# Softmax division moved from GpSimd to ScalarE, and a plan with other transfer rules and weights

## The chip, the cores and the metric

The kernel runs on one core of a Trainium2 chip. Its engines have queues of their own and run them in order: TensorE (PE), VectorE (DVE), ScalarE (ACT), GpSimd (POOL) and SyncE (SP), which issues most transfers (DMA). The metric is the device time of one execution in microseconds (us), less is better.

## The reference

Three parts in a row, all in float32. First attention with 2 batches x 8 heads, 576 rows and a head width of 64, in which each row keeps its 32 largest scores:

```python
scores = scale * np.matmul(q, k.transpose(0, 1, 3, 2))
kth = np.partition(scores, -top_k, axis=-1)[..., -top_k:-top_k + 1]   # top_k = 32
scores = np.where(scores >= kth, scores, -1e9)
attn = np.exp(scores - scores.max(-1, keepdims=True))
attn = attn / (attn.sum(-1, keepdims=True) + 1e-9)
out = np.matmul(attn, v)
```

Then an MLP on the 1152 x 512 result, `h = x @ w_in; (h * cos(h)) @ w_out`, with 2048 hidden columns and weights that come as 64-bit floats. Last a layer of 8 experts: each row goes to the expert with the largest gate logit (a capacity of 288 rows each), `relu(x @ w1) @ w2` with 1024 hidden columns, times the gate's probability.

## The kernel before, in words

The program writes down operations with engine, cost, inputs and outputs (`P.op`, `P.dma`), and a planner (`Plan.emit`) then plays a schedule through with these costs: at each turn it takes, over all engines, the operation that can start first, with ties broken by a rank, and issues it there and then. The order in which it picks is the order in each engine's queue. The ranks come from a table of numbers, `PRM` (the main path) or `FULL` (a fallback that this input does not need). The planner holds VectorE and GpSimd apart for operations marked `port=True`.

Attention is 36 steps (`steps`), each one tile of 128 rows for two heads. A step is:

- `scores` (L477, L483): two halves of matmuls into the one PSUM tile `S`, each copied to `Sp` by ScalarE (L489). There are four `Sp` buffers, so copies run up to three steps ahead.
- `pair_chain`, the search: VectorE takes the larger and the smaller of column pairs (L504, both inputs in SBUF), and alternates "largest 8" (L508, L517, L519) with "replace those 8" (L512).
- `softmax`: the threshold `tb` (GpSimd, L544, L547), a penalty `pen` (ScalarE, L551), its subtraction (GpSimd, L554), the exponential with row sums (ScalarE, L556), a small addition (GpSimd, L559), the reciprocal (VectorE, L561), and the division by the sums, one instruction for each of the two halves (L566): on GpSimd for the first 25 steps and on VectorE for the other 11.
- `products`: nine transposes on TensorE (L581), copies by ScalarE (L583), matmuls with `v`, a copy of the result `xh` on ScalarE (L633) and its rounding rest `xl` on VectorE (L626).

Between these stand the first MLP's parts. `convert` turns 32 tiles of 64-bit weights into float32: a transfer into `wraw` (three buffers), a pass on ScalarE (L384), and then one of two forms. For tiles n < `mul` VectorE does all the rest (L388, L390, L393); for the others ScalarE makes signs (L397), VectorE assembles the bits (L398, L400) and GpSimd multiplies (L403). `split_w` splits 16 of the tiles in a rounded part (L360 on ScalarE, or L358 on GpSimd) and a rest (L354, on VectorE for n < `lod`, else on GpSimd). `layer_in` (L676 to L678, clamp on VectorE, L687), `cosine` (ScalarE, L704), `product` (GpSimd, L712) and `layer_out` (L721) are the MLP; `route` and `place` choose experts. After the last search step TensorE finishes the MLP, rows are gathered by expert, and the experts follow (from L938 on).

```python
eng = DVE if on_dve else POOL
P.op("dve" if on_dve else "pool", 0.38 if on_dve else 0.72, lambda i=i, eng=eng: eng.tensor_scalar(
    T["Sp", s][:, i, :], T["Sp", s][:, i, :], T["sm", s][:, i:i + 1], None, op0=OP.mult),
```

Of the kernel before, what the change touches and what calls it, by code (L numbers as in the profile page):

```python
# [12 lines left out]
AF = mybir.ActivationFunctionType  # L13
OP = mybir.AluOpType
# [5 lines left out]
T = B * S  # L20
# [21 lines left out]
FEWER = 1023.4  # L42


PRM = dict(nd=25, mul=3, c0=-0.572, c1=0.444, c2=-12.204, c3=0.071, sm=-5.344, pr=-0.287, sc=3.303, mx=-11.706, co=9.279, lo=11.63, ro=7.045, tb=-26.596, ga=3.034, lod=6, pc=2, lv=7.781, sw=22.44, s1=1.478)
FULL = dict(nd=36, mul=8, c0=3.627, c1=-2.562, c2=3.854, c3=0.425, sm=1.002, pr=3.858, sc=5.283, mx=0.736, co=8.685, lo=1.174, ro=7.507, tb=11.194, ga=4.52, lod=4, pc=0, lv=2.808, sw=1.416, s1=0.894)


class Plan:
# [56 lines left out]
    def emit(self):  # L106
        ops = self.ops
        for i, o in enumerate(ops):
            for d in o["deps"]:
                ops[d]["succ"].append(i)  # L110
            o["n"] = len(o["deps"])
        free = {}
        for pool, shape, dtype, bufs, tag, gate in self.rings.values():
            free.setdefault(tag, [(0.0, n) for n in range(bufs)])
        line = {}
        for o in sorted(ops, key=lambda o: o["rank"]):
            for k in o["new"]:
                line.setdefault(self.rings[k[0]][4], []).append(k)
        cand, clock, table, at, kind = {}, {}, [None], {}, [None]
        columns = {}  # L120

        held = {"dve": 0.0, "pool": 0.0}
        for e in ("dve", "pool"):
            cand[e] = []
        for i, o in enumerate(ops):
            cand.setdefault(o["eng"], [])
            clock.setdefault(o["eng"], 0.0)
            if o["n"] == 0:
                cand[o["eng"]].append(i)
        left = len(ops)  # L130
        while left:
            best = None
            for e, c in cand.items():
                pick, early = None, None
                opts = []
                for i in c:
                    o = ops[i]
                    s = max(clock[e], o["est"])
                    if o["port"]:
                        s = max(s, held["pool" if e == "dve" else "dve"])  # L140
                    need = {}
                    ok = True
                    for k in o["new"]:
                        f = free[self.rings[k[0]][4]]
                        n = need.get(id(f), 0)
                        tag = self.rings[k[0]][4]
                        if n >= len(f) or tag not in self.mixed and k not in line[tag][:n + 1]:
                            ok = False
                            break
                        s = max(s, sorted(f)[n][0])  # L150
                        need[id(f)] = n + 1
                    if ok:
                        other = o["table"] is not None and o["table"] != table[0]
                        opts.append((s, (o["rank"][0] + self.other * other, o["rank"][1]), i))
                if not opts:
                    continue
                m = min(opts)[0]
                s, _, i = min((x for x in opts if x[0] <= m + 0.02), key=lambda x: x[1])
                if best is None or s < best[0]:
                    best = (s, e, i)  # L160
            if best is None:
                self.stuck(cand)
            s, e, i = best
            o = ops[i]
            cand[e].remove(i)
            for k in o["new"]:
                pool, shape, dtype, bufs, tag, gate = self.rings[k[0]]
                f = free[tag]
                at[k] = min(f)[1]
                f.remove(min(f))  # L170
                line[tag].remove(k)
                self.T[k] = pool().tile(list(shape), dtype, name=k[0], tag=f"{tag}.{at[k]}", bufs=1)
            cost = o["cost"]
            if o["table"] is not None and o["table"] != table[0]:
                table[0] = o["table"]
                cost += 1.3
            if e == "pe":
                if o["kind"] != kind[0]:
                    kind[0] = o["kind"]
                    cost += 0.09  # L180

                k = int(s / 3.4133)
                columns[k] = columns.get(k, 0.0) + cost * 2400 * o["duty"]
                if columns.get(k - 1, 0.0) < 3060:
                    cost *= 2
            o["start"], o["end"] = s, s + cost
            clock[e] = o["end"]
            if o["port"]:
                held[e] = o["end"]
            o["fn"]()  # L190
            left -= 1
            for j in o["succ"]:
                q = ops[j]
                lat = o["lat"]
                if lat is None:
                    lat = 0.28 if (e, q["eng"]) == ("act", "pe") else 0.0 if e == q["eng"] == "pe" else self.LAT[e]
                q["est"] = max(q["est"], o["end"] + lat)
                q["n"] -= 1
                if q["n"] == 0:
                    cand[q["eng"]].append(j)  # L200
            for k in o["tiles"]:
                self.users[k] -= 1
                if self.users[k] == 0:
                    end = o["end"] + (self.LAT[e] if o["lat"] is None else o["lat"])
                    free[self.rings[k[0]][4]].append((end, at[k]))
# [41 lines left out]
def forward(ctx, lasting, tc, kq, vn, vs_, w_in, w_out, w_gate, w1, w2, out, paired):  # L247
    nc = tc.nc
    PE, ACT, DVE, POOL, SP = nc.tensor, nc.scalar, nc.vector, nc.gpsimd, nc.sync
    prm = PRM if paired else FULL  # L250
    P = Plan(prm["tb"])
    T = P.T
# [99 lines left out]
    def subtract(on_dve, dve, pool, args, r, w):  # L352
        eng, cost = (DVE, dve) if on_dve else (POOL, pool)
        P.op("dve" if on_dve else "pool", cost, lambda: eng.tensor_tensor(op=OP.subtract, **args()), r=r, w=w, port=True)  # L354
# [10 lines left out]
    def convert(n):  # L365

        kt = (("wt", "wt3", "wt2", "wt", "wt3", "wt2")[n % 6], n)
        kr = ("wraw2" if n % 3 else "wraw", n)
        kf = slot_of(n)
        if n < 16:  # L370
            u, kc = divmod(n, 4)
            src, r0, c0 = w_in, kc * 128, u * 512
        else:
            src, r0, c0 = w_out, (n - 16) * 128, 0

        def full():
            return T[kf] if n < 16 else T["wo", 0][:, n - 16, :]

        def bits(t):
            return t.bitcast(I32)  # L380

        last = P.dma(0.5, 2.1, lambda: SP.dma_start(
            T[kr], src[r0:r0 + 128, 2 * c0:2 * c0 + 1024].rearrange("p (n t) -> p n t", t=2)), w=[kr])
        P.op("act", 0.56, lambda: ACT.activation(T[kt], T[kr][:, :, 1].bitcast(F32), AF.Copy, scale=2.0 ** -112),  # L384
             r=[kr], w=[kt])
        if n < prm["mul"]:

            P.op("dve", 0.34, port=True, fn=lambda: DVE.tensor_scalar(bits(full()), bits(T[kt]), 3, None,  # L388
                                                                      op0=OP.logical_shift_left), r=[kt], w=[kf])
# [6 lines left out]
        else:  # L396
# [3 lines left out]
            P.op("dve", 0.60, port=True, fn=lambda: DVE.scalar_tensor_tensor(  # L400
                bits(T[kt]), T[kr][:, :, 0], 29, bits(T[kt]), op0=OP.logical_shift_right,
                op1=OP.bitwise_or), r=[kr], w=[kt])
            P.op("pool", 1.23, lambda: POOL.tensor_tensor(out=full(), in0=T[kt], in1=full(), op=OP.mult), r=[kt],  # L403
                 w=[kf])
        return last

    def split_w(n):

        idx = divmod(n, 4)
        hi, lo, w = ("wh", idx), ("wl", idx), ("ws", idx)  # L410
        rounded(n >= 16 - prm["pc"], 0.52, 0.59, lambda: (T[hi], T[w]), r=[w], w=[hi])
        subtract(n < prm["lod"], 0.6, 1.23, lambda: dict(out=T[lo], in0=T[w], in1=T[hi]),
                 r=[w, hi], w=[lo])


# [35 lines left out]

    def load_kq(b, hp):
        k = ("kq", (b, hp))
        P.dma(0.5, 2.5, lambda: SP.dma_start(T[k], kq[b, hp]), w=[k])

    def load_v(b, hp):
        kv = ("v", (b, hp))
        P.dma(0.5, 1.4, lambda: SP.dma_start(T[kv], vn[b, hp]), w=[kv])

    def load_vs(b, g, i):  # L460
        kv = ("v", (b, "s", g, i))
        P.dma(0.5, 1.4, lambda: SP.dma_start(T[kv], vs_[b, 2 * g + i]), w=[kv])

    def scores(s, i):

# [73 lines left out]
    def softmax(s):  # L539
# [21 lines left out]
        P.op("dve", 0.08, lambda: DVE.reciprocal(T["sm", s][:, 0:2], T["sm", s][:, 2:4]), r=[("sm", s, 2)],  # L561
             w=[("sm", s, 3)])
        for i in range(2):
            on_dve = s >= prm["nd"]
            eng = DVE if on_dve else POOL
            P.op("dve" if on_dve else "pool", 0.38 if on_dve else 0.72, lambda i=i, eng=eng: eng.tensor_scalar(  # L566
                T["Sp", s][:, i, :], T["Sp", s][:, i, :], T["sm", s][:, i:i + 1], None, op0=OP.mult),
                r=[("sm", s, 3)], w=[("Sp", s, i)], port=True)

    def products(s):  # L570
        kind, b, j, hp = steps[s]
# [82 lines left out]
    def layer_in(t, u):  # L654
# [29 lines left out]
        def angle():  # L684
            return T["ur", (t, u // 2)][:, u % 2]
        if paired:
# [4 lines left out]
             w=[ku])  # L691
        P.op("dve", 0.34, lambda: DVE.tensor_scalar(T[kn], angle(), MAGIC, MAGIC, op0=OP.add, op1=OP.subtract), r=[ku],
             w=[kn])
        P.op("pool", 1.23, lambda: POOL.tensor_tensor(out=angle(), in0=angle(), in1=T[kn], op=OP.subtract), r=[kn],
             w=[ku])

    def cosine(t):
# [430 lines left out]
```

## Time and profile before

| | |
|---|---|
| time, median of 3 runs | 738.34 us (737.53 to 738.88) |
| the profiled execution's own time | 738.23 us |
| its span, in which all instructions lie | 736.4 us |
| VectorE busy | 558.1 us, 76% |
| TensorE busy | 604.3 us, 82% |
| ScalarE busy | 469.1 us, 64% |
| GpSimd busy | 348.6 us, 47% |

Busy times are averages over stages with different limits, so the stages are read apart. Times in rows are in microseconds from the span's start. An instruction's row shows its start, its duration, and in brackets how long its engine had been idle before it and what ended that. Durations of neighbours overlap a little, so the distance from one start to the next is what an instruction costs its queue. Matmul ends are modelled. Time that an instruction spends waiting inside its engine counts as busy.

### The profile page before, as it was taken

What the parts mean: (1) busy time and instruction counts of PE and PEld (TensorE: products, weight loads), DVE (VectorE), ACT (ScalarE), POOL (GpSimd) and SP (SyncE); (2) the same over time, 40 slices, a digit from 0 to 9 for tenths busy, and PEclk for the clock granted to TensorE, in tenths of its full rate; (3) what the DMA queues carried; (4) which work ended last, traced back from release to release, by engine and by line L of the source; (5) the groups of instructions that cost most, each with busy time, mean ns of one, the idle gap of its engine ahead of it and who ended that gap; (6) DMA issues with size and microseconds to landing.
All of it is one profiled execution on the core that took longest, in us unless ns stands there. A gap on an engine that the chain in (4) does not pass through costs nothing.

```text
span 736.4 us, 11076 instructions
## 1 busy us (share of the span) xinstructions
PE 604.3 (82%) x3611; PEld 437.4 (59%) x3611; DVE 558.1 (76%) x1646; ACT 469.1 (64%) x956; POOL 348.6 (47%) x370
## 2 busy tenths in 40 slices
PE   1223576788799898999999999999945999999995
PEld 0102354554476574566666676667534888888883
DVE  3898999898789997989899993555322888889631
ACT  3564777767558677758777876466312777778631
POOL 3356878789989786767445453123200001101111
PEclk9998569779889999999999999999965999999998
DMA  9644332146031110100000000444203577777200
GB/s 343 218 145 143 115 91 80 31 161 229 1 96 53 36 54 19 36 19 15 16 1 1 1 16 1 165 145 148 86 15 131 186 243 236 250 244 238 98 17 15
DMA packets 29636, 76.24 MB, mean 104 GB/s; under 512 B 3966, under 2 KB 3966, under 8 KB 29568
## 3 DMA queue, kind: packets, MB, share of 16 engines
q1 hardware_dynamic: 27824, 70.68, 28.9%
q0 software_dynamic: 1744, 4.76, 1.7%
q8 instruction: 30, 0.49, 0.3%
q14 instruction: 38, 0.31, 0.1%
HBM read 63.52 MB, written 12.69 MB: 103 GB/s over the span
## 4 chain that ended last, share of the span: by engine, by line
PE 44%; DVE 28%; POOL 11%; ACT 7%; issue 4%; DMA 4%; SPq 1%; POOLq 0%; DVEq 0%; ACTq 0%
PE yp L1001 10%; PE x L721 9%; PE hp L970 7%; POOL Sp L566 7%; DVE W L508 7%; DVE C L512 6%; DVE C L504 4%; PE hp L972 3%; POOL Sp L554 3%; PE h L676 2%; DVE wt L400 2%; DVE W L517 2%; PE pt L581 2%; PE h L677 2%; PE h L678 2%
## 5 line engine op out<-in xcount | busy, mean ns | idle before, releaser
L721 PE MATMUL x<-wo,hs 128*128 128x512 f32 x288 | 138.8, 603 | 1.4 <-POOL hs L712 1.4
L508 DVE MAX8 W<-C 128x8 f32<-128x288 f32 x288 | 117.9, 446 | 0.9
L554 POOL TENSOR_TENSOR Sp<-Sp,pen 128x576 f32<-128x576 f32 x72 | 96.2, 1336 | 38.6 <-ACT pen L551 37.7
L581 PE MATMUL pt<-ident,Sp 128*128 128x128 f32 x324 | 60.8, 311 | 56.9 <-POOL Sp L566 52.6
L938 DVE TENSOR_TENSOR wl<-raw,wh 128x512 fp32r<-128x512 f32 x128 | 90.5, 741 | 19.9 <-ACT wh L936 16.3
L581 PEld LDWEIGHTS pt<-ident,Sp 128*128 128x128 f32 x324 | 39.5, 154 | 93.8 <-POOL Sp L566 71.0
L512 DVE MATCH_REPLACE8 C<-W,C 128x288 f32<-128x288 f32 x216 | 94.0, 441 | 0.0
L566 POOL TENSOR_SCALAR Sp<-Sp,sm 128x576 f32<-128x576 f32 x50 | 89.6, 1801 | 8.7 <-DVE sm L561 8.4
L477 PE MATMUL S<-kq 64*128 64x288 f32 x256 | 57.6, 532 | 41.7 <-ACT Sp L489 32.7
L1007 POOL DMA_INDIRECT out_dram<-ot,ti x16 | 15.2, 949 | 160.4 <-ACT xgs L958 103.3
L936 ACT ACTIVATE wh<-raw 128x512 fp32r<-128x512 f32 x128 | 74.2, 622 | 10.2 <-DMA raw<-in_w_dram 6.1
L676 PE MATMUL h<-xh,wh 128*128 128x256 f32 x256 | 79.8, 312 | 0.0
L721 PEld LDWEIGHTS x<-wo,hs 128*128 128x128 f32 x288 | 48.9, 190 | 45.7 <-issue 41.9
L970 PE MATMUL hp<-xgs,wh 128*128 128x384 f32 x256 | 75.6, 366 | 0.0
L677 PE MATMUL h<-xl,wh 128*128 128x256 f32 x256 | 72.7, 284 | 0.0
L678 PE MATMUL h<-xh,wl 128*128 128x256 f32 x256 | 72.5, 283 | 0.0
L712 POOL TENSOR_TENSOR hs<-hs,ur 128x512 f32<-128x512 f32 x36 | 48.7, 1365 | 50.0 <-ACT ur L704 50.0
L583 ACT ACTIVATE PT<-pt 128x384 f32<-128x384 f32 x108 | 49.8, 484 | 33.8 <-PE pt L581 33.2
L556 ACT ACTIVATE Sp<-Sp,tb 128x576 f32<-128x576 f32 x72 | 55.8, 775 | 23.0 <-POOL Sp L554 22.8
L504 DVE TENSOR_TENSOR C<-Sp 128x576 f32<-128x576 f32 x72 | 69.2, 961 | 1.6 <-ACT Sp L489 0.8
L1001 PE MATMUL yp<-wh,hc 128*128 128x512 f32 x192 | 67.9, 402 | 0.0
L551 ACT ACTIVATE pen<-Sp,tb 128x576 bf16<-128x576 f32 x72 | 55.2, 767 | 18.8 <-POOL tb L544 18.6
(139 smaller groups left out, 1413.0 us busy)
## 6 DMA issues: line engine op xcount, KB each, us to landing
raw<-in_w_dram SPq DMA_DIRECT2D x64, 512.0 KB
wraw<-in_w_out_dram SPq DMA_DIRECT2D x16, 512.0 KB
wraw<-in_w_in_dram SPq DMA_DIRECT2D x16, 512.0 KB
xs<-z SPq DMA_DIRECT2D x1, 4680.0 KB
kq<-in_kq_dram SPq DMA_DIRECT2D x8, 576.0 KB
v<-in_vn_dram SPq DMA_DIRECT2D x8, 320.0 KB
v<-in_vs_dram SPq DMA_DIRECT2D x8, 320.0 KB
out_dram<-z SPq DMA_DIRECT2D x1, 2304.0 KB
```

Of the source, the lines that this page charges most:

```text
L504: DVE.tensor_tensor(out=T["C", s], in0=x[:, :, 0:HS], in1=x[:, :, HS:S], op=op)
L508: P.op("dve", 0.365, lambda r=r, i=i: DVE.max(T["W", s][:, i, LIST[r]:LIST[r] + 8], T["C", s][:, i, :]), r=[("C", s, i)], w=[("W", s, i)])
L512: P.op("dve", 0.42, lambda r=r, i=i: DVE.match_replace(T["C", s][:, i, :], T["W", s][:, i, LIST[r]:LIST[r] + 8], T["C", s][:, i, :], NEG), ...
L554: P.op("pool", 1.34, lambda i=i, kp=kp: POOL.tensor_tensor(out=T["Sp", s][:, i, :], in0=T["Sp", s][:, i, :], in1=T[kp], op=OP.subtract), r ...
L566: P.op("dve" if on_dve else "pool", 0.38 if on_dve else 0.72, lambda i=i, eng=eng: eng.tensor_scalar(T["Sp", s][:, i, :], T["Sp", s][:, i, ...
L581: PE.transpose(T[kp][:, c * 128:(c + 1) * 128], P2[:, cc * 128:(cc + 1) * 128], ident)
L676: PE.matmul(o, hi, a, start=(kc == 0), stop=False, skip_group_check=True)
L677: PE.matmul(o, hi, b, start=False, stop=False, skip_group_check=True)
L721: P.op("pe", 0.86, lambda f=f, a=a: PE.matmul(T["x2", t], T[kh][:, a:a + 128], T["wo", 0][:, f, :], start=(f == 0), stop=(f == 15)), r=[kh ...
L938: P.op("dve", 0.6, lambda a=a, hi=hi, lo=lo: DVE.tensor_tensor(out=T[lo], in0=T[kr][:, a * 512:(a + 1) * 512], in1=T[hi], op=OP.subtract), ...
L970: PE.matmul(T[kp][:, 0:2 * MAIN], T[ka][:, c:c + 128], x.rearrange("p a n -> p (a n)"), start=(kc == 0), stop=False, skip_group_check=True)
L1001: PE.matmul(T[kp], x, w, start=(fc + n == 0), stop=(fc == 7 and n == len(uses) - 1))
```

## The change

The division by the sums runs on ScalarE (a copy with a scale for each row) in the first 22 steps (`na`) and on VectorE in the other 14; none is left on GpSimd. In the planner, transfers that have been issued are taken in the order of issue, whichever could start first, and SyncE may run no more than 2.5 us ahead of the transfers' clock. Costs of transfers are smaller (2.1 becomes 1.65 for weights, for instance), two costs on GpSimd larger. The table `PRM` has other numbers: among them `mul` is 1 for 3, `lod` 10 for 6 and `pc` 0 for 2, and all of the ranks differ.

```diff
-PRM = dict(nd=25, mul=3, ..., lod=6, pc=2, lv=7.781, sw=22.44, s1=1.478)
+PRM = dict(na=22, mul=1, ..., lod=10, pc=0, lv=11.745, sw=6.214, s1=0.597)
...
                     if o["port"]:
                         s = max(s, held["pool" if e == "dve" else "dve"])
+                    if e == "sp":
+                        s = max(s, clock["dma"] - 2.5)
...
-                s, _, i = min((x for x in opts if x[0] <= m + 0.02), key=lambda x: x[1])
+                if e == "dma":
+                    s, _, i = min(opts, key=lambda x: (ops[x[2]]["est"], x[2]))
+                else:
+                    s, _, i = min((x for x in opts if x[0] <= m + 0.02), key=lambda x: x[1])
...
-        last = P.dma(0.5, 2.1, lambda: SP.dma_start(
+        last = P.dma(0.45, 1.65, lambda: SP.dma_start(
...
-        P.dma(0.5, 2.5, lambda: SP.dma_start(T[k], kq[b, hp]), w=[k])
+        P.dma(0.45, 1.85, lambda: SP.dma_start(T[k], kq[b, hp]), w=[k])
...
         for i in range(2):
-            on_dve = s >= prm["nd"]
-            eng = DVE if on_dve else POOL
-            P.op("dve" if on_dve else "pool", 0.38 if on_dve else 0.72, lambda i=i, eng=eng: eng.tensor_scalar(
-                T["Sp", s][:, i, :], T["Sp", s][:, i, :], T["sm", s][:, i:i + 1], None, op0=OP.mult),
-                r=[("sm", s, 3)], w=[("Sp", s, i)], port=True)
+            if s < prm["na"]:
+                P.op("act", 0.67, lambda i=i: ACT.activation(T["Sp", s][:, i, :], T["Sp", s][:, i, :], AF.Copy,
+                                                             scale=T["sm", s][:, i:i + 1]),
+                     r=[("sm", s, 3)], w=[("Sp", s, i)])
+                continue
+            P.op("dve", 0.39, lambda i=i: DVE.tensor_scalar(T["Sp", s][:, i, :], T["Sp", s][:, i, :],
+                                                            T["sm", s][:, i:i + 1], None, op0=OP.mult),
+                 r=[("sm", s, 3)], w=[("Sp", s, i)], port=True)
```

Where instructions stand now is read from each engine's queue in program order. In the changed kernel line numbers are up to 8 higher. The first place is ScalarE at the program's start, after the first two weight tiles. Before (`wt` and `wo` are the passes over a weight tile in `wraw`, L384 and L397; `Sp` is a copy of half a step's scores, L489):

```order
L384 ACTIVATE wt<-wraw 128x512
L397 ACTIVATE wo<-wraw 128x512
L489 ACTIVATE Sp<-S 128x2x288
L384 ACTIVATE wt_170<-wraw_147 128x512
L397 ACTIVATE wo<-wraw_147 128x512
L489 ACTIVATE Sp<-S 128x2x288
L384 ACTIVATE wt_182<-wraw_157 128x512
```

Now, with the passes on L389 and L402, the copy on L494 and the penalty on L556:

```order
L389 ACTIVATE wt<-wraw 128x512
L402 ACTIVATE wo<-wraw 128x512
L494 ACTIVATE Sp<-S 128x2x288 x7
L556 ACTIVATE pen<-Sp,tb 128x576
L389 ACTIVATE wt_233<-wraw_149 128x512
L402 ACTIVATE wo<-wraw_149 128x512
L494 ACTIVATE Sp<-S 128x2x288
```

Seven score copies, of three and a half steps, and the first penalty stand ahead of the fourth weight tile, where one copy stood.

The second place is GpSimd around step 7, with the small addition (`sm`), the subtraction (`Sp<-Sp,pen`), weight products (`ws`) and the division (`Sp<-Sp,sm`). Before:

```order
L559 TENSOR_SCALAR sm<-sm 128x2
L554 TENSOR_TENSOR Sp<-Sp,pen 128x576
L566 TENSOR_SCALAR Sp<-Sp,sm 128x576 x2
L403 TENSOR_TENSOR ws<-wt_730,ws 128x512
L554 TENSOR_TENSOR Sp<-Sp,pen 128x576
L559 TENSOR_SCALAR sm<-sm 128x2
L403 TENSOR_TENSOR ws<-wt,ws 128x512
L566 TENSOR_SCALAR Sp<-Sp,sm 128x576 x2
```

Now (subtraction on L559, addition on L564, products on L408):

```order
L564 TENSOR_SCALAR sm<-sm 128x2
L408 TENSOR_TENSOR ws<-wt_723,ws 128x512
L559 TENSOR_TENSOR Sp<-Sp,pen 128x576
L408 TENSOR_TENSOR ws<-wt_750,ws 128x512
L559 TENSOR_TENSOR Sp<-Sp,pen 128x576
```

The divisions are gone; subtractions and weight products stand next to each other.

The third place is ScalarE at the same stage of the program. Before, with the rounded weights `wh` (L360) and the output's copy `xn` (L633) beside the passes named above:

```order
L384 ACTIVATE wt_730<-wraw_588 128x512
L489 ACTIVATE Sp<-S 128x2x288
L360 ACTIVATE wh<-ws 128x512
L633 ACTIVATE xn<-av 128x128
L556 ACTIVATE Sp,sm<-Sp,tb 128x576
L489 ACTIVATE Sp<-S 128x2x288
L397 ACTIVATE ws<-wraw_732 128x512
L551 ACTIVATE pen<-Sp,tb 128x576
```

Now (exponential on L561, penalty on L556, division on L570):

```order
L561 ACTIVATE Sp,sm<-Sp,tb 128x576
L365 ACTIVATE wh<-ws 128x512
L556 ACTIVATE pen<-Sp,tb 128x576
L570 ACTIVATE Sp<-Sp,sm 128x576 x2
L389 ACTIVATE wt<-wraw 128x512
L402 ACTIVATE ws<-wraw 128x512
L641 ACTIVATE xn<-av 128x128
```

The two divisions of a step stand between a penalty and the passes over the next weight tile.

## Rows read from the trace of the kernel before

**Rows 1.** The profile's page, its first line.

```profile
span 736.4 us, 11076 instructions
```

**Rows 2.** Stages: length; busy PE, PEld, DVE, ACT, POOL (instructions); clock, DMA, GB/s.

```profile
24.00:149.10 125.10, 64.28 (x377) 43.26 (x377) 118.14 (x310) 86.22 (x166) 86.97 (x78) 0.82 0.34 109
149.10:301.10 152.00, 134.64 (x843) 88.45 (x844) 135.21 (x420) 105.11 (x201) 132.00 (x128) 0.91 0.23 79
301.10:445.80 144.70, 139.54 (x957) 97.64 (x956) 136.41 (x453) 107.94 (x209) 80.25 (x98) 1.00 0.04 13
445.80:541.00 95.20, 91.69 (x491) 59.70 (x489) 40.73 (x98) 50.45 (x90) 23.73 (x25) 1.00 0.31 106
541.00:736.40 195.40, 170.14 (x935) 146.83 (x935) 119.80 (x358) 110.09 (x276) 18.41 (x21) 0.92 0.49 158
```

**Rows 3.** Timeline of ScalarE, 8 to 25 us: start, duration, instruction, idle before.

```profile
10.36 0.65 ACT L489 ACTIVATE Sp<-S 128x576 f32<-128x576 f32 x1 [1.61 <-PE S L477]
20.49 0.66 ACT L384 ACTIVATE wt<-wraw 128x512 f32<-128x512 f32 x1 [9.48 <-DMA wraw<-in_w_out_dram]
...
21.61 0.63 ACT L489 ACTIVATE Sp<-S 128x576 f32<-128x576 f32 x1
```

**Rows 4.** Timeline of TensorE, 8 to 25 us.

```profile
11.06 1.33 PE L477 MATMUL S<-kq 64*128 64x288 f32 x4 [0.75 <-ACT Sp L489]
```

**Rows 5.** Timeline of VectorE, 20 to 25 us.

```profile
23.96 0.74 DVE L504 TENSOR_TENSOR C<-Sp 128x576 f32<-128x576 f32 x1
```

**Rows 6.** VectorE's waits, 149.1 to 301.1 and 24 to 149.1: total, times, longest.

```profile
DVE xl L626 <- ACT xh L633: 8.3, 6, 2.8
...
DVE ws L388 <- ACT wt L384: 2.6, 2, 1.8
```

**Rows 7.** GpSimd's groups, 24 to 445.8: count, busy, mean ns, idle before.

```profile
L566 POOL TENSOR_SCALAR Sp<-Sp,sm 128x576 f32<-128x576 f32 x50 | 89.6, 1801 | 8.7 <-DVE sm L561 8.4 <-DVE W L519 0.3
```

**Rows 8.** VectorE's groups, 24 to 445.8.

```profile
L504 DVE TENSOR_TENSOR C<-Sp 128x576 f32<-128x576 f32 x72 | 69.2, 961 | 1.6 <-ACT Sp L489 0.8
...
L400 DVE SCALAR_TENSOR_TENSOR wt<-wraw,wt 128x512 int32<-128x512 int32 x25 | 21.1, 853 | 0.0
L398 DVE TENSOR_SCALAR wt<-wt 128x512 int32<-128x512 int32 x25 | 17.4, 704 | 3.9 <-ACT wt L384 3.8
...
L566 DVE TENSOR_SCALAR Sp<-Sp,sm 128x576 f32<-128x576 f32 x20 | 11.1, 599 | 0.0
...
L354 DVE TENSOR_TENSOR wl<-ws,wh 128x512 fp32r<-128x512 f32 x6 | 4.1, 683 | 0.0
L393 DVE SCALAR_TENSOR_TENSOR ws<-wt,ws 128x512 int32<-128x512 int32 x3 | 4.0, 1360 | 0.0
```

**Rows 9.** Single lines of VectorE: shortest, median and longest duration in ns.

```profile
L504 DVE TENSOR_TENSOR C<-Sp x72: 740/758/1843, 24.0 to 442.9; 128x576 f32<-128x576 f32 x72
...
L400 DVE SCALAR_TENSOR_TENSOR wt<-wraw,wt x29: 666/679/1771, 5.9 to 145.2; 128x512 int32<-128x512 int32 x29
...
L398 DVE TENSOR_SCALAR wt<-wt x29: 400/422/1497, 5.5 to 142.1; 128x512 int32<-128x512 int32 x29
```

**Rows 10.** Timeline of GpSimd and VectorE, 56 to 62 and 168 to 172 us.

```profile
56.63 5.04 POOL L566 TENSOR_SCALAR Sp<-Sp,sm 128x576 f32<-128x576 f32 x2
...
58.72 0.75 DVE L504 TENSOR_TENSOR C<-Sp 128x576 f32<-128x576 f32 x1
...
168.49 1.28 POOL L554 TENSOR_TENSOR Sp<-Sp,pen 128x576 f32<-128x576 f32 x1
...
169.13 1.25 DVE L504 TENSOR_TENSOR C<-Sp 128x576 f32<-128x576 f32 x1
```

**Rows 11.** Timeline of ScalarE, 60 to 83 us.

```profile
68.19 0.77 ACT L551 ACTIVATE pen<-Sp,tb 128x576 bf16<-128x576 f32 x1
68.85 0.66 ACT L384 ACTIVATE wt<-wraw 128x512 f32<-128x512 f32 x1
```

**Rows 12.** ScalarE's waits, 24 to 149.1 us.

```profile
ACT PT L583 <- PE pt L581: 14.3, 10, 3.7
```

More of the change, by code (lines that the diff above doesn't have):

```diff
@@ L42 @@
 FEWER = 1023.4
-PRM = dict(nd=25, mul=3, c0=-0.572, c1=0.444, c2=-12.204, c3=0.071, sm=-5.344, pr=-0.287, sc=3.303, mx=-11.706, co=9.279, lo=11.63, ro=7.045, tb=-26.596, ga=3.034, lod=6, pc=2, lv=7.781, sw=22.44, s1=1.478)
-FULL = dict(nd=36, mul=8, c0=3.627, c1=-2.562, c2=3.854, c3=0.425, sm=1.002, pr=3.858, sc=5.283, mx=0.736, co=8.685, lo=1.174, ro=7.507, tb=11.194, ga=4.52, lod=4, pc=0, lv=2.808, sw=1.416, s1=0.894)
+PRM = dict(na=22, mul=1, c0=-4.505, c1=0.411, c2=-30.35, c3=1.14, sm=-6.538, pr=0.274, sc=2.931, mx=-1.055, co=1.204, lo=5.261, ro=7.18, tb=9.729, ga=4.016, lod=10, pc=0, lv=11.745, sw=6.214, s1=0.597)
+FULL = dict(na=12, mul=8, c0=3.627, c1=-2.562, c2=3.854, c3=0.425, sm=1.002, pr=3.858, sc=5.283, mx=0.736, co=8.685, lo=1.174, ro=7.507, tb=11.194, ga=4.52, lod=4, pc=0, lv=2.808, sw=1.416, s1=0.894)
 class Plan:
@@ L402, in convert @@
                 op1=OP.bitwise_or), r=[kr], w=[kt])
-            P.op("pool", 1.23, lambda: POOL.tensor_tensor(out=full(), in0=T[kt], in1=full(), op=OP.mult), r=[kt],
+            P.op("pool", 1.27, lambda: POOL.tensor_tensor(out=full(), in0=T[kt], in1=full(), op=OP.mult), r=[kt],
                  w=[kf])
@@ L411, in split_w @@
         rounded(n >= 16 - prm["pc"], 0.52, 0.59, lambda: (T[hi], T[w]), r=[w], w=[hi])
-        subtract(n < prm["lod"], 0.6, 1.23, lambda: dict(out=T[lo], in0=T[w], in1=T[hi]),
+        subtract(n < prm["lod"], 0.6, 1.27, lambda: dict(out=T[lo], in0=T[w], in1=T[hi]),
                  r=[w, hi], w=[lo])
@@ L453, in load_kq @@
         k = ("kq", (b, hp))
-        P.dma(0.5, 2.5, lambda: SP.dma_start(T[k], kq[b, hp]), w=[k])
+        P.dma(0.45, 1.85, lambda: SP.dma_start(T[k], kq[b, hp]), w=[k])
     def load_v(b, hp):
         kv = ("v", (b, hp))
-        P.dma(0.5, 1.4, lambda: SP.dma_start(T[kv], vn[b, hp]), w=[kv])
+        P.dma(0.45, 1.05, lambda: SP.dma_start(T[kv], vn[b, hp]), w=[kv])
     def load_vs(b, g, i):
         kv = ("v", (b, "s", g, i))
-        P.dma(0.5, 1.4, lambda: SP.dma_start(T[kv], vs_[b, 2 * g + i]), w=[kv])
+        P.dma(0.45, 1.05, lambda: SP.dma_start(T[kv], vs_[b, 2 * g + i]), w=[kv])
     def scores(s, i):
@@ L693, in layer_in @@
              w=[kn])
-        P.op("pool", 1.23, lambda: POOL.tensor_tensor(out=angle(), in0=angle(), in1=T[kn], op=OP.subtract), r=[kn],
+        P.op("pool", 1.27, lambda: POOL.tensor_tensor(out=angle(), in0=angle(), in1=T[kn], op=OP.subtract), r=[kn],
              w=[ku])
```

## The prediction

> **What bounds the kernel now.** I read the time by stage first [rows 2]: 24.0 to 445.8 us is the top-32 search (the attention steps), 445.8 to 541.0 the rest of the first MLP, and from 541.0 to the end the experts. In the search VectorE is busy 118.1 of 125.1, 135.2 of 152.0 and 136.4 of 144.7 us, 389.8 of 421.8 in all. TensorE shows as busy in the later stretches too, but its matmul ends are modelled and overlap. In the last two stages TensorE is busy 91.7 of 95.2 and 170.1 of 195.4 us and its order hardly changes. So I ask when VectorE's last search instruction ends (445.8 now, where I cut the stages; the last L504 starts at 442.9 [rows 9], and step 9 begins at the cut at 149.1), and let what follows move with it unchanged.
>
> Second, the timeline of the start [rows 3 to 5]. TensorE begins step 0's second half of scores at 11.06 and is through 1.33 us later, at 12.39. ScalarE is free from 11.01, yet the next instruction in its queue is the first pass over a weight tile whose transfer lands late: it sits idle 9.48 us and starts at 20.49. The copy of the waiting scores stands two places behind it and runs at 21.61. The search (L504) starts only at 23.96. VectorE, which bounds the next 420 us, therefore loses about 11 us before it begins.
>
> Third, VectorE's 32.0 us of idle time in the search: 7.0, 16.8 and 8.3 us in the three stretches [rows 2]. In the middle stretch, where GpSimd is busy 132.0 of 152.0 us, the largest wait is for the copy of the attention output on ScalarE (8.3 us) [rows 6]. That copy is behind transposes that wait for the division on GpSimd, L566, which takes 1.80 us a time, 50 times [rows 7].
>
> Fourth, time in which VectorE counts as busy but waits for GpSimd [rows 8, 9]: L504 takes 961 ns on average and 758 in the median (72 times: 14.6 us), L398 704 and 422 (25 times: 7.1 us), L400 853 and 679 (25 times: 4.4 us), L393 1360 against the 679 of the same operation (3 times: 2.0 us). That is 28 us.
>
> **The change, part by part.** The sum is made against the profiled execution, 738.2 us (span 736.4 [rows 1]); the median of the runs shown is 738.3, so nothing separates them.
>
> *The start.* ScalarE's new order has seven score copies ahead of the first late weight tile. The second copy can start at 12.39, ends 0.65 later, and L504 starts at about 13.1 instead of 23.96: -10.9. The plan's new rule on transfers is what moves it; the transfers themselves hardly change order. Behind step 0, VectorE's second step soon wants weight tiles that ScalarE passes over only after the seven copies: at one matmul pair and one copy, 2.1 us, each, the seventh runs at about 22.8 (10.36 + 6 x 2.1), so the tile is ready at about 25, when VectorE is in the middle of step 1. I take 1.0 us of wait; the bounds are 0 and 5, the second being half of the gain.
>
> *VectorE's work between first and last search instruction.* Two L398 and one L400 that ran ahead of the search now follow it: 2 x 0.42 + 0.68 = 1.5 us. Four more splits of weights (L354, 0.683): 2.7. Six more divisions (28 for 22, at 0.599): 3.6. Two weight tiles fewer in the three-operation form (0.42 + 0.68 + 0.68) and two more in the form with two (0.42 + 0.68): -1.4. Sum +6.4. With the two tiles go two thirds of L393's extra 2.0 us and of the 2.6 us for which VectorE waited on ScalarE ahead of L388 [rows 6]: -3.0. So +3.4.
>
> *GpSimd.* It loses 50 divisions, 89.6 us of the 299.2 that it is busy from 24.0 to 445.8 [rows 2, 7], four splits and two roundings, and gains two weight products. Steps 9 to 22, which fill the middle stretch, divide 28 times, 50 us of its 132.0 there: it falls from 87% busy to 54%. The two divisions of a step then take 2 x 0.66 us on ScalarE instead of 2 x 1.80, so transposes and the copy that VectorE waits for come over 2 us earlier per step. I take half of the 16.8 us of idle time away, -8; the bounds are -16.8 (all) and 0. The last stretch keeps its 8.3: from step 25 on the division was on VectorE already.
>
> *ScalarE.* The trace has no division there. The nearest row is L551, the same 128x576 pass with a per-row operand: it starts at 68.19 and the next instruction at 68.85, so it takes 0.66 us of the queue [rows 11]; 44 of them are 29 us. Up to step 9 (149.1) the load is 86.2 us [rows 2], plus three weight tiles that now follow the start, 3 x 1.12 (two passes from 20.49 to 21.61, [rows 3]), plus 18 x 0.66, plus two passes at 0.56: 103 us in about 125. That is 82%, against 69% before. What speaks for it holding: 14.3 us of ScalarE's own waits in this stretch are for transposes [rows 12], which the GpSimd division held back. I charge +2; the bounds are 0 and the 16 of the third rival.
>
> *Waits for GpSimd inside VectorE's instructions.* At 56.63 GpSimd starts two L566 that last until 61.67; L504 at 58.72 runs beside them in 0.75 us, the undisturbed time. At 169.13 it starts 0.64 us into L554, an operation with two inputs, and takes 1.25 [rows 10]. So the 28 us belong to the two-input operations, which stay: 72 L554 and 31 instead of 29 weight products. I take 0; the bounds are -8 and +5, the first being L566's share of GpSimd's time, 89.6 of 299.2, of those 28 us, the second the half of it that other chance meetings could add. The Trainium skill (SBUF — State Buffer, Who interferes with whom) says that a GpSimd operation that starts first gets the shared port pair for its whole instruction and the other engine blocks. For L554 the trace agrees; for L566 it does not: 0.75 us in the midst of 5.04.
>
> *After the last step.* TensorE's, GpSimd's and VectorE's orders are the same but for a few neighbours, and the expert stage has its gathers slightly earlier beside a TensorE that is full: 0, within 2 either way. Search steps that come faster could run into TensorE; but they do so in the middle stretch, where it is busy 134.6 of 152.0 us even with its ends modelled late, and the last stretch, where it shows 139.5 of 144.7, keeps its pace.
>
> Sum: -10.9 + 1.0 + 3.4 - 8 + 2 + 0 = -12.5. 738.2 - 12.5 = 725.7, say **725 us**.
>
> **The rivals.**
> - *Only the start is won.* VectorE's idle time is not GpSimd's doing but that of the long way from search to output copy, and moves to another wait. For it: the wait names ScalarE, not GpSimd. Against: the division is the slowest link of that way. Then -10.9 + 1.0 + 3.4 = -6.5: 731.7 us.
> - *GpSimd's division held the port as well.* The 28 us fall by L566's share, 8.4 us: 717 us. It is the skill's rule quoted above. Against it stands the undisturbed L504 of [rows 10]; for it, that other plans may line the two engines up better, which would look the same in the time.
> - *ScalarE becomes the bound, and the kernel slower.* Place: its queue up to step 9, at 103 us of work. If it still waits as long as before there (125.1 - 86.2 = 39 us), the stretch takes 142 us instead of about 125, +16, and nothing is won later since VectorE then waits for ScalarE: -10.9 + 1.0 + 3.4 + 16 = +9.5, 748 us. It decides from about 29 us of ScalarE waiting in that stretch, where the +6.5 eats up the other terms. For it: weights wait for VectorE's passes, these for ScalarE, and each is in order. Against: waits on the GpSimd division go.
> - *The change doesn't do what it says at the start*: the early copies find their score matmuls waiting for transfers, and L504 stays near 24. Then 3.4 - 8 + 2 = -2.6, 735.6 us. Against: step 0's scores were ready at 12.39 in this trace.
>
> **How the numbers follow.** Chances: forecast 0.53 (its own range 718 to 732), only the start 0.17, port 0.14, ScalarE 0.11, start not won 0.05. 0.2% of 738 is 1.5 us, about what a measurement tells from no change. Faster by more: nearly all of the first three and half of the last, 0.84; slower by more: the ScalarE case and a bit of the second, 0.11; the same 0.05. The range runs from 709 to 736: below, it holds the port case with the idle time's further bound (717 - 8 = 709); above, the start-only case and the one in which the start isn't won; it leaves out the ScalarE case and the ends.
>
> **What would show it.** Right: the first L504 near 13; step 9 starting near 138 (149.1 - 10.9) give or take 4; VectorE's idle time from there to step 22 at 10 us or less; the last search instruction near 433; the division on ScalarE at 0.76 us a row; the 28 us of L504, L398, L400 and L393 still between 20 and 33; the span behind the search at 290.6 us (736.4 - 445.8) within 2. Wrong: a late first L504; ScalarE over 90% busy with VectorE waiting for L398's input; L504 down to near 758 ns on average, which would be the port; a longer rest of the first MLP, which would mean that TensorE had become the bound.

## The result

The changed kernel takes 705.1 us (704.2 to 707.0, 4 runs) against 738.2 us (737.5 to 738.9): a ratio of 0.9555, 95% interval 0.9534 to 0.9577. The direction was right. The size was not: 33 us were won where 13 were forecast, and 705 lies below the range.

The profiled execution by stage; columns as in [rows 2], cut at the same events: step 9 begins at 132.8 us, step 23 at 270.0, the search ends at 412.8.

```profile
13.80:132.80 119.00, 64.36 (x375) 44.44 (x375) 117.90 (x309) 93.30 (x179) 69.31 (x67) 0.90 0.44 145
132.80:270.00 137.20, 129.92 (x867) 86.24 (x867) 131.90 (x425) 125.87 (x241) 77.88 (x94) 0.96 0.26 87
270.00:412.80 142.80, 135.73 (x938) 95.19 (x935) 139.63 (x459) 109.13 (x211) 67.48 (x90) 1.00 0.04 14
412.80:510.00 97.20, 92.25 (x493) 60.04 (x491) 40.77 (x99) 50.30 (x90) 24.80 (x26) 0.98 0.31 103
510.00:705.10 195.10, 171.76 (x935) 147.88 (x935) 117.46 (x358) 110.98 (x276) 20.05 (x20) 0.92 0.49 158
```

The search took 421.8 us and takes 399.0, and VectorE is now busy in all but 9.5 us of it (1.1, 5.3 and 3.2 by stretch; 7.0, 16.8 and 8.3, 32.0 in all, before). GpSimd went from 132.0 of 152.0 us in the middle stretch to 77.9 of 137.2, ScalarE from 105.1 to 125.9: 92%, and yet VectorE hardly waits.

VectorE's start on its timeline, where [rows 5] had 23.96:

```profile
13.85 0.76 DVE L509 TENSOR_TENSOR C<-Sp 128x576 f32<-128x576 f32 x1 [2.91 <-ACT Sp L494]
```

Its groups in the search, to be held against [rows 8] (L509 was L504, L405 L400, L403 L398, L359 L354):

```profile
L509 DVE TENSOR_TENSOR C<-Sp 128x576 f32<-128x576 f32 x72 | 64.5, 896 | 3.7 <-ACT Sp L494 2.9
L405 DVE SCALAR_TENSOR_TENSOR wt<-wraw,wt 128x512 int32<-128x512 int32 x28 | 20.4, 742 | 0.0
L403 DVE TENSOR_SCALAR wt<-wt 128x512 int32<-128x512 int32 x28 | 18.7, 676 | 0.4 <-ACT wt L389 0.4
L359 DVE TENSOR_TENSOR wl<-ws,wh 128x512 fp32r<-128x512 f32 x10 | 8.9, 895 | 0.0
```

Three means fell, L509 from 961 to 896, L405 from 853 to 742 and L403 from 704 to 676; that of L359 rose from 683 to 895. Last, VectorE's largest wait in the search, for [rows 6], and the division on ScalarE:

```profile
DVE xl L634 <- ACT xh L641: 3.0, 7, 0.9
```

```profile
L570 ACT ACTIVATE Sp<-Sp,sm 128x576 f32<-128x576 f32 x44 | 31.6, 767 | 10.3 <-DVE sm L566 10.3
```

For all runs I split the search's length in three: *idle* is the length less VectorE's busy time; *port waits* are what VectorE's passes over SBUF tiles (one or two inputs, over 380 ns, all lines) last beyond the lower quartile of their own line; *own work* is what remains. The *rest* is the span behind the search. That a line's lower quartile is its undisturbed time is assumed, and a line that occurs once shows no wait (in the changed kernel one pass of L393 lasts 1524 ns); other ways of taking the quartile move port waits and own work by about 1 us against each other. In us, from the profiled executions:

| kernel | search starts | length | own work | port waits | idle | rest |
|---|---|---|---|---|---|---|
| before | 24.0 | 421.8 | 353.0 | 36.8 | 32.0 | 290.6 |
| changed | 13.8 | 399.0 | 359.7 | 29.8 | 9.5 | 292.3 |
| difference | -10.2 | -22.8 | +6.7 | -7.0 | -22.5 | +1.7 |

The differences of start, own work, port waits, idle time and rest add up to the span's: -31.3, 736.4 to 705.1.

### The profile page after: what moved, and what is told of

Same layout as the page of the kernel before. It is cut to its first block, busy times and chain, and to the rows that moved or that the text cites. A ratio compares the mean times of both kernels' runs of the same rounds, so it can differ in the third digit from the quotient of the medians.

```text
span 705.1 us, 11071 instructions
## 1 busy us (share of the span) xinstructions
PE 596.7 (85%) x3611; PEld 434.8 (62%) x3611; DVE 553.4 (78%) x1654; ACT 496.0 (70%) x1004; POOL 265.2 (38%) x316
## 4 chain that ended last, share of the span: by engine, by line
PE 41%; DVE 34%; ACT 16%; DMA 3%; issue 3%; POOL 1%; SPq 1%; POOLq 0%; DVEq 0%; ACTq 0%
PE yp L1009 11%; DVE W L513 9%; DVE C L517 8%; PE hp L978 7%; PE x L729 7%; DVE C L509 4%; PE hp L980 3%; ACT Sp L561 2%; ACT pen L556 2%; DVE W L522 2%; DVE wt L405 2%; ACT Sp L570 2%; ACT Sp L494 2%; PE h L684 2%; DVE Sp L574 2%
## 5 line engine op out<-in xcount | busy, mean ns | idle before, releaser
L559 POOL TENSOR_TENSOR Sp<-Sp,pen 128x576 f32<-128x576 f32 x72 | 97.5, 1354 | 64.8 <-ACT pen L556 64.5
L589 PE MATMUL pt<-ident,Sp 128*128 128x128 f32 x324 | 56.4, 304 | 38.6 <-ACT Sp L570 31.6
L589 PEld LDWEIGHTS pt<-ident,Sp 128*128 128x128 f32 x324 | 40.4, 154 | 66.1 <-ACT Sp L570 41.0
L684 PE MATMUL h<-xh,wh 128*128 128x256 f32 x256 | 78.0, 305 | 0.5 <-ACT hs L691 0.4
L1015 POOL DMA_INDIRECT out_dram<-ot,ti x16 | 17.9, 1117 | 159.0 <-ACT ot L1024 124.8
L1009 PE MATMUL yp<-wh,hc 128*128 128x512 f32 x192 | 70.1, 405 | 0.0
L509 DVE TENSOR_TENSOR C<-Sp 128x576 f32<-128x576 f32 x72 | 64.5, 896 | 3.7 <-ACT Sp L494 2.9
L980 PE MATMUL hp<-xgs,wl 128*128 128x192 f32 x256 | 65.5, 256 | 0.0
L561 ACT ACTIVATE Sp<-Sp,tb 128x576 f32<-128x576 f32 x72 | 55.7, 774 | 13.1 <-POOL Sp L559 12.9
L556 ACT ACTIVATE pen<-Sp,tb 128x576 bf16<-128x576 f32 x72 | 55.3, 768 | 6.3 <-POOL tb L549 5.5
L591 ACT ACTIVATE PT<-pt 128x384 f32<-128x384 f32 x108 | 48.5, 483 | 12.1 <-PE pt L589 12.0
```

The source lines that it names most:

```text
L509: DVE.tensor_tensor(out=T["C", s], in0=x[:, :, 0:HS], in1=x[:, :, HS:S], op=op)
L559: P.op("pool", 1.34, lambda i=i, kp=kp: POOL.tensor_tensor(out=T["Sp", s][:, i, :], in0=T["Sp", s][:, i, :], in1=T[kp], op=OP.subtract), r ...
L589: PE.transpose(T[kp][:, c * 128:(c + 1) * 128], P2[:, cc * 128:(cc + 1) * 128], ident)
L684: PE.matmul(o, hi, a, start=(kc == 0), stop=False, skip_group_check=True)
L980: PE.matmul(T[kp][:, 0:MAIN], T[kb][:, c:c + 128], x[:, 0], start=False, stop=(kc == 3), skip_group_check=True)
L1009: PE.matmul(T[kp], x, w, start=(fc + n == 0), stop=(fc == 7 and n == len(uses) - 1))
```

## The experiments

Each ran beside the kernel before on its chip; ratios are to that, with 95% intervals.

**Transfer rule alone.** Kernel before, with the planner's two rules and the transfers' costs of the change.

```diff
+                    if e == "sp":
+                        s = max(s, clock["dma"] - 2.5)
...
+                if e == "dma":
+                    s, _, i = min(opts, key=lambda x: (ops[x[2]]["est"], x[2]))
```

> The kernel before with the new rule on transfers and their new costs alone: old ranks, old mul, lod and pc, division on GpSimd as before. Start theory: the seven score copies stand ahead of the late weight tile here too, so the first L504 moves from 24.0 to about 13.8 us and everything behind follows: 738 - 10 = 728 us, with VectorE idle for about 32 us in the search as before. Rival, that the start is given back (weights come later, and the first steps wait for them): 735 to 738 us with the first L504 at 14.

Measured: 734.5 us, 0.9949 (0.9932 to 0.9966). The search starts early, at 13.57, and VectorE's largest wait (total, times, longest) shows some of what became of it:

```profile
DVE sm L566 <- POOL sm L564: 14.3, 11, 2.5
```

Of the 10.4 us by which the search starts earlier, 3.4 remain at its end. VectorE now waits for GpSimd's small addition (L564), which stands in one queue with the slow divisions. That these delay it isn't shown: in the ten of these waits that last over 0.25 us, a division is never the instruction just ahead of the addition. Idle time rose from 32.0 to 42.5. The rival was nearer.

**Old order, division issued to ScalarE.** The planner still counts 0.72 us on GpSimd, so every other instruction keeps its place.

```diff
-            P.op("dve" if on_dve else "pool", ..., lambda i=i, eng=eng: eng.tensor_scalar(...),
+            def divide(i=i, on_dve=on_dve):
+                x, r = T["Sp", s][:, i, :], T["sm", s][:, i:i + 1]
+                if on_dve:
+                    DVE.tensor_scalar(x, x, r, None, op0=OP.mult)
+                else:
+                    ACT.activation(x, x, AF.Copy, scale=r)
+            P.op("dve" if on_dve else "pool", 0.38 if on_dve else 0.72, divide,
```

> The kernel before with the plan untouched (the planner still thinks of the division as 0.72 us on GpSimd, so every other instruction keeps its place), but the 50 divisions are issued to ScalarE. Engine theory (GpSimd's slow division, twice 1.8 us a step, made VectorE wait): VectorE's idle time falls from 32 to 10 to 15 us although the order is old, the start stays at 24.0: 738 - 18 = about 720 us. Plan theory (an order worked out with wrong costs and transfers made VectorE wait): the order is as wrong as before, idle time stays above 25 us: 732 to 738 us. ScalarE theory: its queue, now longer by 29 us that the plan does not know of, delays VectorE: above 740 us.

Measured: 711.1 us, 0.9617 (0.9596 to 0.9638). That is below all three theories. Most of the change's gain (0.0383 of 0.0445) comes from where 50 instructions run, with the start at 24.3; all other instructions run in the same order in every queue. VectorE's L504, and the middle and last stretch:

```profile
L504 DVE TENSOR_TENSOR C<-Sp 128x576 f32<-128x576 f32 x72 | 62.6, 869 | 1.6 <-ACT Sp L489 0.8
```

```profile
139.70:276.00 136.30, 126.12 (x837) 82.76 (x838) 127.99 (x419) 120.43 (x227) 84.69 (x99) 0.96 0.25 88
276.00:420.00 144.00, 141.40 (x963) 98.77 (x962) 134.28 (x453) 114.17 (x220) 68.02 (x90) 1.00 0.04 14
```

Idle time fell by 10.1 us only, less than the engine theory said: in the middle stretch from 16.8 to 8.3, while the last one has 9.7 for 8.3. Another 15.0 us are port waits (36.8 to 21.8), which none of these theories had. Beside a running division VectorE can have lost only 3.7 of them: in the trace of before, 29 passes of VectorE began beside one, 16 undisturbed and 13 with 3.7 us lost in all. The larger part is meetings with the subtraction L554: 30 of them cost 21.0 us before, 19 cost 12.1 here, with the same 72 subtractions and the same order.

**New order, division issued to GpSimd.** The reverse, on the changed kernel.

```diff
-                P.op("act", 0.67, lambda i=i: ACT.activation(..., AF.Copy, scale=T["sm", s][:, i:i + 1]),
+                P.op("act", 0.67, lambda i=i: POOL.tensor_scalar(..., T["sm", s][:, i:i + 1], None, op0=OP.mult),
```

> The changed kernel with its plan untouched (division planned for ScalarE at 0.67 us), but the 44 divisions of the first 22 steps are issued to GpSimd, where one takes 1.8 us. Engine theory: GpSimd is as full as before, VectorE's idle time goes back from 10 to about 30 us: 705 + 20 = 725 us. Plan theory in its strong form (the other ranks and the transfer rule did it, not the place of the division): 705 to 712 us. If the waits inside VectorE's instructions grow by 8 us or more, the GpSimd division holds the port after all.

Measured: 756.6 us, 1.0239 (1.0222 to 1.0256), slower than either kernel. GpSimd's division and VectorE's largest wait:

```profile
L570 POOL TENSOR_SCALAR Sp<-Sp,sm 128x576 f32<-128x576 f32 x44 | 87.3, 1993 | 6.6 <-DVE sm L566 5.6 <-DVE W L524 1.0
```

```profile
DVE xl L634 <- ACT xh L641: 23.0, 16, 3.5
```

Idle time went to 53.3 us, far past the 30 expected, and the time past both theories; port waits rose by 3.3 only. A division takes 1993 ns on the mean where it took 1801 before: 17 of the 44, each with a pass of VectorE running beside it, took 1.97 to 3.36 us, where the 16 without one took 1.71 to 1.73. So VectorE delays the division, by 11.9 us in all, while VectorE itself lost 3.8 us beside divisions. My reading is that the new order leans on a quick division: the output's rest L634 stands close behind it.

**Division left on GpSimd, but told truly.** The planner gets the cost that the trace shows, and no longer keeps the division apart from VectorE.

```diff
-            P.op("dve" if on_dve else "pool", 0.38 if on_dve else 0.72, ..., port=True)
+            P.op("dve" if on_dve else "pool", 0.38 if on_dve else 1.72, ..., port=on_dve)
```

> The kernel before with the division left on GpSimd but told to the planner as it is: 1.72 us for 0.72, and not kept apart from VectorE's port operations. Plan theory (the wrong cost made an order in which VectorE waits): idle time falls below 15 us, 720 to 725 us. Engine theory (GpSimd is simply full and slow, whatever the order): 733 to 740 us with about 30 us idle. The start stays at 24.0 in both.

Measured: 726.8 us, 0.983 (0.981 to 0.985): neither. By stage:

```profile
24.20:137.10 112.90, 56.50 (x319) 36.45 (x319) 110.10 (x305) 77.17 (x150) 84.10 (x72) 0.85 0.36 121
137.10:288.10 151.00, 137.79 (x910) 92.37 (x909) 135.55 (x427) 113.80 (x219) 141.15 (x136) 0.96 0.23 79
288.10:433.90 145.80, 137.70 (x964) 96.81 (x963) 134.06 (x452) 106.77 (x208) 76.94 (x96) 1.00 0.04 13
```

The middle stretch is as before, 151.0 us with GpSimd busy for 141.2, which fits a full engine that sets it. The first stretch is 12 us shorter, with 2.8 us of idle time for 7.0. Idle time in all is 30.0, near the 32.0 before; port waits are 25.5, 11.3 less, with the division still on GpSimd.

**Keys first.** The changed kernel with the first keys ahead of the weights.

```diff
     constants()
+    R("rank", -40.0)
     load_kq(0, 0)
```

> The changed kernel with one more move: the transfer of the first keys and queries gets the lowest rank and goes ahead of the three weight tiles (1.5 MB) that stood in front of it. If the search's length is set by VectorE's own work, whatever starts earlier ends earlier: first L509 at about 10 us for 13.8, 705 - 3.5 = 701.5 us. Rival: the early start is lost again in the steps behind it, as most of it was in the run with the transfer rule alone: 704 to 707 us.

Measured: 713.5 us, 0.9679 (0.9644 to 0.9714), 8 us slower than the changed kernel and past both theories, though the search starts at 12.0. A pass on VectorE met GpSimd even ahead of it (L405, 1.64 us at 10.45). L509 up to step 9, in the changed kernel and here, and one pass of the expert choice here:

```profile
L509 DVE TENSOR_TENSOR C<-Sp 128x576 f32<-128x576 f32 x19 | 16.5, 870 | 3.0 <-ACT Sp L494 2.9
L509 DVE TENSOR_TENSOR C<-Sp 128x576 f32<-128x576 f32 x18 | 21.4, 1190 | 0.3 <-ACT Sp L494 0.3
404.13 4.32 DVE L755 TENSOR_SCALAR onehot<-iota,small 128x8 bf16<-128x8 f32 x1
```

L509 lasts 1190 ns instead of 870, and port waits are 35.8 us for 29.8. Of the 6.0 us more, 3.9 are the single pass L755: it takes 0.23 us in three of its four other places in this run, and here it began 0.69 us into a two-input operation of GpSimd and ended only with the fourth of a row of four. Idle time (+3.0) and the rest (+2.3) grew too. An earlier start is worth nothing if more than it is lost behind it.

**New division and rule, old numbers.** The changed kernel with the old table and `na=22`.

> The changed kernel with the old numbers (ranks, mul, lod, pc), so new division and new transfer rule alone. If the division's place made VectorE's idle time and port waits go, and the start adds its 10 us: 700 to 708 us, idle time below 20 us. If the new numbers were needed for it: 712 us or more, since the run on the old order with the division on ScalarE had 711.

Measured: 703.0 us, 0.9518 (0.9495 to 0.9541). The new numbers brought nothing: they stand at 0.9555 (0.9534 to 0.9577). Their order has 7.0 us more port waits (29.8 for 22.8), 2.4 more own work, and a rest shorter by 3.3.

**Division alone.** Old numbers, old transfer rule and costs; the division as in the change.

> The kernel before with the division alone (ScalarE for 22 steps, VectorE for 14, planned as such), old numbers, old transfer rule and costs. Engine theory: like the run that issued the divisions to ScalarE behind the planner's back, 706 to 714 us, with the start at 24 us and port waits near 22 us. If a plan that knows of the division loses ScalarE's time elsewhere: 718 us or more.

Measured: 707.6 us, 0.9597 (0.9563 to 0.9630), with the start at 24.0. By stage:

```profile
24.00:139.80 115.80, 71.86 (x422) 48.47 (x423) 112.05 (x312) 95.71 (x182) 75.40 (x72) 0.90 0.41 138
139.80:269.90 130.10, 119.52 (x795) 77.53 (x793) 126.06 (x418) 117.73 (x225) 73.75 (x91) 0.96 0.21 74
269.90:408.60 138.70, 136.10 (x950) 96.28 (x950) 135.59 (x459) 108.71 (x213) 68.98 (x90) 1.00 0.04 14
```

By itself the division gives 0.0403 of the change's 0.0445. This is the shortest search of all, 384.6 us, with 18.9 us of port waits and 10.9 idle (3.8, 4.0 and 3.1 by stretch). With the rule it starts 10.3 us earlier and is 8.1 longer (own work +2.5, port waits +3.9, idle +1.6), and its rest is 1.2 shorter: 3.4 us are left in the span, 4.6 in the median. The rest is 296.8 us here, 6 longer than before.

**Planner without the port.** Three kernels in which the planner no longer keeps VectorE and GpSimd apart: the changed one, the division alone, and the kernel before.

```diff
-        o = dict(..., port=eng == "pool" if port is None else port, ...)
+        o = dict(..., port=False, ...)
```

> The changed kernel with a planner that no longer keeps VectorE and GpSimd apart. If the planned distance is what lowers the port waits once GpSimd keeps to its plan, they go from 30 us to the 37 of the kernel before or more: 712 us and up. If it does nothing (meetings are chance): 703 to 708 us with about 30 us.

> The run with the division alone (707.6 us, port waits 18.9 us), with a planner that doesn't keep VectorE and GpSimd apart. Theory of the kept plan: once GpSimd runs no slower than planned, the planned distance works, so without it port waits go back to 30 us or more: 717 to 724 us. Rival (the waits fell because GpSimd is less full, whatever the plan): port waits stay below 23 us, 705 to 712 us.

> The kernel before, with the same edit. Theory of the kept plan: with the division at 0.72 us in the plan and 1.80 on GpSimd, the planned distance was worth nothing, so taking it away changes little: port waits 34 to 41 us, 735 to 745 us. Rival (the distance worked there too): port waits 45 us or more, 750 us and up.

Measured: 721.9 us, 0.9777 (0.9754 to 0.9801); 746.5 us, 1.0122 (1.0096 to 1.0147); 766.5 us, 1.0399 (1.0370 to 1.0429). Port waits:

| division | planner keeps apart | doesn't | difference |
|---|---|---|---|
| ScalarE, as planned (division alone) | 18.9 | 36.8 | +17.9 |
| ScalarE, as planned (changed kernel) | 29.8 | 33.8 | +4.0 |
| GpSimd, 1.80 for a planned 0.72 (before) | 36.8 | 41.3 | +4.5 |

For the old numbers the port waits are about what the theory of the kept plan says: the distance that is planned works where GpSimd keeps to the plan, and is nearly lost where it runs late. That GpSimd is less full doesn't do it by itself: the 36.8 of the first row, without the distance, are as many as before the change. For the new numbers it was worth little too (33.8 lies between the two expectations), so they use it badly; why isn't settled. The times moved by more than the port waits: in the second kernel idle time rose by 21.5 us, in the third by 17.0, and the theory's times missed in both: 746.5 for 717 to 724, and 766.5 for 735 to 745, where the rival had said 750 and up. The planned distance also orders other things, so these runs don't show it alone.

**28 and 16 steps on ScalarE**, with the old numbers.

```diff
-PRM = dict(na=22, mul=3, ...
+PRM = dict(na=28, mul=3, ...
```

> The changed kernel with old numbers (703.0 us), the division on ScalarE for 28 steps instead of 22. VectorE loses 12 divisions of 0.51 us, 6 us of its own work; ScalarE gains 8 us in a stretch where it is busy for 109 of 143. If VectorE is still the bound: 697 to 700 us. If TensorE has become the bound behind the search: 701 to 704 us with a longer rest.

> The same with 16 steps: VectorE gains 12 divisions, 6 us of work, ScalarE loses 8 us in the stretch from step 9 to 23, where it was busiest. If VectorE is the bound: 707 to 711 us; if ScalarE's queue there held VectorE up: 700 to 704 us.

Measured: 701.2 us, 0.9509 (0.9485 to 0.9534), and 708.5 us, 0.9613 (0.9583 to 0.9643). With 28, VectorE's own work falls by 6.3 us and its idle time rises by 5.3; the end of the search moves by 1.0. In the last stretch (264.8 to 405.4) VectorE is busy for 129.6 of 140.6 us, idle for 11; it no longer sets that stretch alone. The time is that of the TensorE theory, but its longer rest isn't there (294.0 us for 295.6). With 16, own work and port waits rise by 3.1 and 3.9. 28 steps and old numbers are the best version seen, 4 us under the changed kernel; from 22 steps with old numbers it can't be told apart, since the intervals overlap.

All runs, in the same split as above:

| kernel | search starts | length | own work | port waits | idle | rest |
|---|---|---|---|---|---|---|
| rule alone | 13.6 | 428.8 | 356.7 | 29.6 | 42.5 | 290.0 |
| old order, issued to ScalarE | 24.3 | 395.6 | 351.8 | 21.8 | 21.9 | 291.2 |
| new order, issued to GpSimd | 13.6 | 446.9 | 360.6 | 33.1 | 53.3 | 292.0 |
| GpSimd, true cost | 24.2 | 409.6 | 354.2 | 25.5 | 30.0 | 291.0 |
| keys first | 12.0 | 403.7 | 355.4 | 35.8 | 12.5 | 294.6 |
| old numbers | 13.7 | 392.7 | 357.3 | 22.8 | 12.5 | 295.6 |
| division alone | 24.0 | 384.6 | 354.8 | 18.9 | 10.9 | 296.8 |
| changed, no port | 13.7 | 410.5 | 359.8 | 33.8 | 16.9 | 296.0 |
| division alone, no port | 22.4 | 423.9 | 354.8 | 36.8 | 32.4 | 298.2 |
| before, no port | 22.5 | 443.7 | 353.4 | 41.3 | 49.0 | 298.2 |
| 28 steps | 13.3 | 392.0 | 351.0 | 23.2 | 17.8 | 294.0 |
| 16 steps | 13.4 | 399.4 | 360.4 | 26.7 | 12.2 | 292.6 |

## Why the prediction was right in direction and wrong in size

**The step that failed** is the part on GpSimd, with the neighbour on ScalarE: "I take half of the 16.8 us of idle time away, -8", "The last stretch keeps its 8.3", "I charge +2". All of VectorE's idle time was put at 25 to 26 us behind the change; it is 9.5. The term was -22.5 where the forecast had -6.7 (-8, +1.0, +2, and -1.7 of the L388 waits). By stretch the forecast left 8.3, 8.8 and 8.3 us; the runs have 1.1, 5.3 and 3.2.

The prediction gave no row for its half. Moved in an unchanged order, the division takes the middle stretch from 16.8 to 8.3 us, which is the -8 to the place, but it takes only 10.1 us in all, and the last stretch keeps its idle time. What the forecast had at nothing is a plan that knows of the move: with the same numbers, but planned on ScalarE for 22 steps and on VectorE for 14 (division alone), idle time is 10.9 us, another 11.0 less, nearly all of it in the middle and last stretch (4.0 and 3.1 us left for 8.3 and 9.7). Such a plan needs the move: with the division on GpSimd the search has 30.0 to 53.3 us of idle time in all four kernels whose planner keeps the engines apart, whatever the plan; planned on ScalarE or VectorE, 9.5 to 17.8 in six. (In the first stretch a plan with the true cost did nearly as much without the move, 2.8 us.) That a full GpSimd stood behind waits which bear ScalarE's name is a reading of the chain: the output's copy on ScalarE needs the transposes L581 on TensorE (now L589), and these waited for the division, before and now:

```profile
PE pt L581 <- POOL Sp L566: 52.6, 31, 10.8
```

```profile
PE pt L589 <- ACT Sp L570: 31.6, 8, 15.9
```

**The second term that was mis-sized** is the port: "the 28 us belong to the two-input operations, which stay. I take 0", where [rows 10] had shown rightly that a division costs VectorE little. It costs the division more: of the two that the row holds together, the one beside the L504 lasted 3.32 us, where 1.72 is usual.

```profile
58.35 3.32 POOL L566 TENSOR_SCALAR Sp<-Sp,sm 128x576 f32<-128x576 f32 x1
```

The conclusion on the 28 us was wrong: the operations stay, their meetings don't. By that count (mean less 758, 422, 679 and 679 ns for the four lines) 28 us became 18.8; on all lines the change is -7.0 here and -17.9 for the division alone. The bound of -8 was made from the division's share of GpSimd's time, and so from the wrong mechanism; that -7.0 lies within it is luck. Shown is that the waits go when the division leaves GpSimd in an unchanged order, and that plans with and without the distance differ by 17.9 us with the old numbers. That GpSimd's lateness is the link between the two is the reading that fits both, and the 25.5 us of the run with the true cost as well; it stays a reading, since other orders moved port waits by as much as 7 us without it.

**The start** was right to the place (13.85 for 13.1; the first score matmuls, which wait for the first keys, began at 9.71 for 8.98) and in its cause, ScalarE's queue. As a gain of 10.9 us it was too large: taken alone the rule is worth a ratio of 0.9949, some 4 us, and on top of the division 4.6 us by medians. The wait for weight tiles that I charged with 1.0 was 0.4; what takes the rest back is work moved behind the start, port waits and idle time. The two errors had opposite signs.

**VectorE's own work**, +6.4 forecast, was +6.7. **The division on ScalarE** costs 767 ns a row, as L551's row had. **The rest**, 0 within 2, was +1.7. It grows to 298 in other runs, though, so it isn't a constant of the kernel.

**The rivals.** ScalarE as the bound did not come about: up to step 9, where 103 us of work in 125 were forecast, it was busy 93.3 of 119.0 us; in the middle stretch, where it was busiest, 125.9 of 137.2, and there VectorE waited 3.5 us for it. The port rival had the direction and 717 us, but not the cause, and its sign, an L504 near 758 ns on the mean, stayed out: 896. Only the start being won fell with the idle time of 9.5 us, and the start not being won with the 13.85.

## What to carry to other kernels

An engine that is nearly full and runs later than the schedule assumes costs twice: others wait for it, and, as far as the readings above hold, what was placed around it no longer is. Before taking half of a wait, look at what the awaited instruction itself waits for, and how full that engine is. Then plan again for the new place: here that took as much idle time away as the move itself. And an earlier start of the bounding engine is worth what is left at its end, which only a run with that edit alone can tell.

## What had not been expected of the hardware

A one-input pass on GpSimd (L566) lets VectorE's passes, of one input or two, run beside it with at most some 0.46 us lost each; it is the GpSimd pass that gets longer. In the trace of before 26 divisions without such a pass beside them took 1.71 to 1.73 us, and 10 of the other 24 took 1.75 to 3.32. Behind GpSimd's two-input operations, in that trace up to the end of the search, 48 of 51 passes that began more than 0.15 us before the operation's end had to wait, 35.1 us in all. Such a wait need not end with the operation: the 128x8 pass L755 waited through four in a row, 4.32 us. ScalarE at 92% busy over 137 us held VectorE up by 3.5 us.
